# Four linked edits to an attention and two-layer gated feed-forward kernel: rows of a chunk loaded once, omega from two queues, first squares on ScalarE, planner constants

## The chip, the cores and the metric

One core of one Trainium2 chip. The time is device microseconds (us) of one execution; lower is better. Engines: PE (TensorE), DVE (VectorE), ACT (ScalarE), POOL (GpSimd), SP (SyncE, which here only issues DMAs).

## The reference

Attention with random features, then two gated feed-forward blocks, all in float32. B, H, S, D = 4, 8, 576, 64; 128 features; 2304 tokens of width 512; inner width 1536.

```python
scale = 1.0 / np.sqrt(np.sqrt(D))
def phi(x):                       # x is q * scale or k * scale
    proj = np.einsum('bhsd,md->bhsm', x, omega)
    h = proj - np.sum(x * x, axis=-1, keepdims=True) / 2.0
    return np.exp(h - np.max(h, axis=-1, keepdims=True)) / np.sqrt(m)
kv = np.einsum('bhsm,bhsd->bhmd', k_p, v)
z = np.sum(k_p, axis=2)
num = np.einsum('bhsm,bhmd->bhsd', q_p, kv)
out = num / (np.einsum('bhsm,bhm->bhs', q_p, z)[..., None] + 1e-06)
x = out.transpose(0, 2, 1, 3).reshape(B * S, H * D)
x = (silu(x @ w_gate) * (x @ w_val)) @ w_out
return ((x @ w_a) * (x @ w_b)) @ w_out2
```

## The kernel before

The tokens go through in five chunks of 512 (the last has 256). A chunk needs the attention of its tokens, for four pairs of heads (NP = 4), and then the two feed-forward blocks (layer(c, 0) and layer(c, 1), lines 756 and on). Every feed-forward product is made of three matmuls, since a float32 factor is split into a high and a low part in the format fp32r (lines 768 to 770). The input x and the inner rows h are split by ACT (high part: xh, hh) and DVE (low part: xl, hl), the weights likewise (wh on line 748, wl through sub on line 320).

Weights arrive as float64 bits, 512 KB a tile, on SP's queue (line 724); two ACT operations (727, 730) and two DVE operations (733, 736) make float32 of them. Half of the tiles are converted in the first chunk, half in the first and again in the second; a converted tile is written back to DRAM (kept, line 742), and later chunks load that (line 746).

The attention of the next chunk runs beside the feed-forward blocks of the present one. For a pair of heads, keys() (478) and queries() (537) load the transposed rows (xT, by loads() on 464), the tokens (kt, qt) and values (vt), all on SP's queue, and call features() (364). That squares the tokens in place on POOL (line 376), sums them on DVE (378, 381), projects the rows on PE (411 or 436), takes maxima on DVE (446), forms a bias (449, 453) and takes exponentials on ACT (458). The keys' features are then multiplied with the values on PE (ps_kv, line 495).

How the rows are multiplied with omega depends on the chunk:

- WHOLE (chunk 0): float32 rows times bd, a 128x256 block-diagonal of omega, one matmul a tile (line 436). bd is filled by two DMAs of omega from ACT's queue (338) and two memsets (341).
- SPLIT (chunk 1): rows split in high and low part (rs, 396 and 399), times bdh and bdl (353, 355), three matmuls.
- STACKED (chunks 2 to 4): for each head of the pair, one tile rs holds the high part of its 64 rows on one half of the partitions and the low part on the other, times oms (both parts of omega side by side, copied by POOL on line 359), one matmul a tile (411). For this loads() fetches the 64 rows of a head twice, to both halves of a tile xT; ACT rounds all 128 partitions (388) and POOL subtracts on the upper half (391, through 320). A pair takes four tiles xT, two for the keys and two for the queries; the ring has four (261).

The order of the instructions on each engine is not written by hand. All operations are recorded with an engine, an estimated duration and a due time, and Plan.order() (97) plays them through: whichever engine is free next takes, of its operations whose inputs are there by then, the one with the earliest due time. An operation's result is there SIGNAL us after its end; a DMA occupies a common pipe at RATE (in MB per us). ACT pays TABLE for a change of its function table. The due times of the layers begin at ALONE and are spaced by the estimated PE time (at(), 331); a raw weight load may not be planned earlier than EARLY us ahead of its due time. Estimates of POOL are 0.2 + 0.0023 us an element, of ACT 0.09 + n/1200, of DVE 0.07 + n/960. The order found is then issued; on the chip each engine and queue keeps to it and waits on semaphores.

Of the kernel before, what the change touches and what calls it, by code (L numbers as in the profile page):

```python
# [9 lines left out]
F32 = mybir.dt.float32  # L10
# [46 lines left out]
class Plan:  # L57
# [5 lines left out]

    SIGNAL = 0.06
    TABLE = 1.4
    RATE = 0.26

    def __init__(self):  # L70
        self.ops = []
# [25 lines left out]
    def order(self):  # L97
# [4 lines left out]
            for b in o.bufs:  # L102
                b.left = b.ops
        engines = (PE, ACT, DVE, POOL, SP)
        free = dict.fromkeys(engines, 0.0)
        coming = {e: [] for e in engines}
        waiting = {e: [] for e in engines}
        held = {}
# [86 lines left out]
def attention_moe_moe(ctx: ExitStack, tc: tile.TileContext, qT, kT, q, k, v, omegaT,  # L195
# [124 lines left out]
        eng.tensor_tensor(out=out, in0=a, in1=hi.bitcast(F32), op=ALU.subtract)  # L320


    ALONE = 44.0
    EARLY, LATE = 26.0, 3.0
    FFN, BESIDE = 0.2258 / 512, 28.0
    n_ffn = 3 * (2 * NF * KD + NF * KD)
# [8 lines left out]

    def constants():
        for h in range(2):
            on(ACT, dma(32), -1e6, lambda h=h: nc.scalar.dma_start(
                out=bd.tile[h * D:(h + 1) * D, h * M:(h + 1) * M], in_=omegaT),
                writes=[(bd, (h, h))])  # L340
            on(DVE, dve(M), -1e6, lambda h=h: nc.vector.memset(
                bd.tile[h * D:(h + 1) * D, (1 - h) * M:(2 - h) * M], 0.0),
                writes=[(bd, (h, 1 - h))])
        on(DVE, dve(1), -1e6, lambda: nc.vector.memset(warm.tile, 0.0), writes=[(warm,)])
        on(ACT, act(1), -1e6, lambda: nc.scalar.activation(
            out=warm.tile, in_=warm.tile, func=AF.Exp), writes=[(warm,)], table="exp")
        on(POOL, dict(pace=0.6), -1e6, lambda: make_identity(nc, ident.tile), writes=[(ident,)])
        for i, t in enumerate(r_vt.tiles):
            on(POOL, pool(650), -1e6, lambda t=t: nc.gpsimd.memset(t, 1.0), writes=[(ones, i)])
        for i, t in enumerate(r_kp.tiles):  # L350
            on(POOL, pool(128), 20, lambda t=t: nc.gpsimd.memset(
                t[:, :, 1].bitcast(F32), 0.0), writes=[(zeros, i)])
        on(DVE, dve(256), 20, lambda: nc.vector.tensor_copy(bdh.tile, bd.tile),
           reads=[(bd, *bd.state)], writes=[(bdh,)])
        on(DVE, dve(256), 20, lambda: sub(nc.vector, bdl.tile, bd.tile, bdh.tile),
           reads=[(bd, *bd.state), (bdh,)], writes=[(bdl,)])
        for i, x in enumerate((bdh, bdl)):
            for h in range(2):
                on(POOL, pool(M), 25, lambda i=i, x=x, h=h: nc.gpsimd.tensor_copy(
                    oms.tile[h * D:(h + 1) * D, i], x.tile[h * D:(h + 1) * D, h * M:(h + 1) * M]),  # L360
                    reads=[(x,)], writes=[(oms, (i, h))])


    def features(rT, tok, nt, step, f, due, length, how, psum):

# [5 lines left out]

        def square():
            x = tok.tile[:, 0:nt].rearrange("p t c -> p (t c)")
            nc.gpsimd.tensor_tensor(out=x, in0=x, in1=x, op=ALU.mult)
        on(POOL, pool(nt * P), due - 4, square, writes=[(tok,)])
        on(DVE, dve(nt * P), due - 2, lambda: nc.vector.tensor_reduce(
            out=s.tile[:, 0:nt], in_=tok.tile[:, 0:nt].rearrange("p t (h d) -> p t h d", h=2),
            op=ALU.add, axis=AX.X), reads=[(tok,)], writes=[(s,)])  # L380
# [4 lines left out]
        for h in range(2 if how == STACKED else 0):  # L385
            rs = r_rs.buf()
            stacks.append(rs)
            on(ACT, act(width), due - 4, lambda rs=rs, h=h: nc.scalar.activation(  # L388
                out=rs.tile[:, 0:width], in_=rT[h].tile[:, 0:width], func=AF.Copy),
                reads=[(rT[h], *rT[h].state)], writes=[(rs,)])  # L390
            on(POOL, pool(width), due - 3, lambda rs=rs, h=h: sub(
                nc.gpsimd, rs.tile[D:P, 0:width], rT[h].tile[D:P, 0:width],
                rs.tile[D:P, 0:width]), reads=[(rT[h], *rT[h].state)], writes=[(rs,)])
        if how == SPLIT:
            hi, lo = r_rs.buf(), r_rs.buf()
            on(ACT, act(width), due - 4, lambda: nc.scalar.activation(
                out=hi.tile[:, 0:width], in_=rT[0].tile[:, 0:width], func=AF.Copy),
                reads=[(rT[0], *rT[0].state)], writes=[(hi,)])
            on(POOL, pool(width), due - 3, lambda: sub(
                nc.gpsimd, lo.tile[:, 0:width], rT[0].tile[:, 0:width], hi.tile[:, 0:width]),  # L400
                reads=[(rT[0], *rT[0].state), (hi,)], writes=[(lo,)])
        for g in range(0, nt, 2):
            n = min(2, nt - g)
            mx, top, bias = r_mx.buf(), r_top.buf(), r_bias.buf()
# [2 lines left out]
            if how == STACKED:  # L407
                for t in range(g, g + n):
                    ps = psum.buf()
                    for h in range(2):  # L410
                        on(PE, pe(0.12), d, lambda h=h, ps=ps, t=t: nc.tensor.matmul(  # L411
                            ps.tile[:, 256 * h:256 * (h + 1)],
                            lhsT=stacks[h].tile[:, step * t:step * t + P],
                            rhs=oms.tile.rearrange("p t m -> p (t m)"), start=True, stop=True),
                           reads=[(stacks[h],), (oms, *oms.state)], writes=[(ps, h)])

                    def half(i, ps=ps):
                        return ps.tile.rearrange("p (h t m) -> p h t m", h=2, t=2)[:, :, i]
                    on(ACT, act(256, 0, True), d, lambda half=half, t=t: nc.scalar.activation(
                        out=f.tile[:, t], in_=half(0), func=AF.Copy),  # L420
                       reads=[(ps, 0, 1)], writes=[(f, (t, 0), (t, 1))])
                    on(DVE, dve(256), d, lambda half=half, t=t: nc.vector.tensor_tensor(
                        out=f.tile[:, t], in0=f.tile[:, t], in1=half(1), op=ALU.add),
                       reads=[(ps, 0, 1)], writes=[(f, (t, 0), (t, 1))])
                keys_of = [(f, *parts)]
            else:
                ps = psum.buf()
                for i in range(n):
                    def proj(i=i, ps=ps, g=g):
                        c = slice(step * (g + i), step * (g + i) + P)  # L430
                        out = ps.tile[:, 256 * i:256 * (i + 1)]
                        terms = ([(hi.tile[:, c], bdh.tile), (hi.tile[:, c], bdl.tile),
                                  (lo.tile[:, c], bdh.tile)] if how == SPLIT else
                                 [(rT[0].tile[:, c], bd.tile)])
                        for j, (w, x) in enumerate(terms):
                            nc.tensor.matmul(out, lhsT=w, rhs=x, start=j == 0,  # L436
                                             stop=j == len(terms) - 1)
                    on(PE, pe(0.36 if how == SPLIT else 0.45), d, proj,
                       reads=[(hi,), (lo,), (bdh,), (bdl,)] if how == SPLIT else
                       [(rT[0], *rT[0].state), (bd, *bd.state)], writes=[(ps, i)])  # L440
                keys_of = [(ps, *range(n))]

            def h_of(ps=ps, g=g, n=n):
# [17 lines left out]
                   reads=[(bias,)] if how == STACKED else [(bias,), (ps, t - g)],  # L461
                   writes=[(f, (t, h))], table="exp")

    def loads(rT, src, p, due, how, pieces):

        for h, x in enumerate(rT):
            for b, a, z, at_ in pieces:
                for i in range(len(rT)):
                    rows_ = slice(h * D, (h + 1) * D) if how == STACKED else slice(0, P)
                    to = slice(i * D, (i + 1) * D) if how == STACKED else slice(0, P)  # L470
                    on(SP, dma((z - a) / 2 / len(rT)), due - 9, lambda x=x, b=b, a=a, z=z,
                       at_=at_, to=to, rows_=rows_: nc.sync.dma_start(
                           out=x.tile[to, at_:at_ + z - a], in_=src[b, p][rows_, a:z]),
                       writes=[(x, (i, b))])

    sums, spread = {}, {}

    def keys(b, p, due, length, how):

        rT, tok, vt = [r_xT.buf() for _ in range(2 if how == STACKED else 1)], r_kt.buf(), r_vt.buf()  # L480
        loads(rT, kT, p, due, how, [(b, 0, S, 0)])
        on(SP, dma(320), due - 8, lambda: nc.sync.dma_start(out=tok.tile, in_=bass.AP(
            k.tensor, k.offset + (b * S) * DM + p * P, [[DM, P], [TS * DM, KT], [1, P]])),
            writes=[(tok,)])
# [2 lines left out]
                                               [[DM, P], [TS * DM, KT], [1, P]])),  # L487
           reads=[(ones, 0, 1)], writes=[(vt,)])
        f, kv = r_kf.buf(), ps_k.buf()
        features(rT, tok, KT, TS, f, due, length, how, ps_m if how == WHOLE else ps_p)  # L490
        for t in range(KT):
            for h in range(2):
                r = rows[t]
# [43 lines left out]
    def queries(c, p, due, length, how):  # L537
# [1 line left out]
        t0, t1 = spans[c]  # L539
        n = t1 - t0  # L540
        nt = n // P
        rT, tok = [r_xT.buf() for _ in range(2 if how == STACKED else 1)], r_qt.buf()
        loads(rT, qT, p, due, how,
              [(b, max(t0, b * S) - b * S, min(t1, (b + 1) * S) - b * S, max(t0, b * S) - t0)
               for b in range(t0 // S, (t1 - 1) // S + 1)])
        on(SP, dma(n / 2), due - 8, lambda: nc.sync.dma_start(
# [331 lines left out]
```

## Time and profile before

| | |
|---|---|
| median of 3 runs (lowest, highest) | 1073.5 us (1070.06, 1074.39) |
| profiled execution | 1073.3 us, its span 1071.5 us |
| mean granted clock of PE over the span | 0.992 |
| instructions | 16062 |
| DMA traffic | 177.01 MB, mean 165 GB/s |
| ACT table loads | 24 of 1.28 us |

The span is what the profile covers; the execution has 1.8 us around it. A busy time is the sum of the time in which an engine had an instruction running. "idle before <-" names what an engine's instruction waited for last. An entry like xT<-kT reads: written tile <- what is read. A granted clock of 1.00 is the full level, 0.50 the lower.

### The profile page before, as it was taken

The page shows a single profiled execution, that of the slowest core. Times are in us where ns is not written, and L with a number is a line of the kernel's source. Part 1 is how long each engine was busy: PE and PEld are TensorE (multiplying, and loading weights), DVE is VectorE, ACT ScalarE, POOL GpSimd, SP SyncE. Part 2 cuts the span into 40 slices and gives each one's busy share as a digit, 9 for nine tenths or more (in the row PEclk, how much of TensorE's full clock was granted, in tenths as well). Part 3 has the DMA queues.
Part 4 walks back from the last instruction along what each step waited for, and adds up shares of the span by engine and source line. Part 5 has one row for each costly group of instructions (what it writes and reads, how often), then busy time and mean ns, then how long its engine had stood idle before and what let it go on. Part 6 is the DMA issues. An engine that isn't in the chain of part 4 may idle for free.

```text
span 1071.5 us, 16062 instructions
## 1 busy us (share of the span) xinstructions
PE 1044.3 (97%) x5444; PEld 891.2 (83%) x5444; DVE 750.1 (70%) x1441; ACT 686.1 (64%) x1437; POOL 173.3 (16%) x150
## 2 busy tenths in 40 slices
PE   7989999999999999979999999999999999999998
PEld 6868787888888887868888888888888888889998
DVE  5899898999766778979654476885544455536663
ACT  3979987888666668676564456665444445437563
POOL 3220020111100042332400042333000110000000
PEclk9999999999999999989999999999999999999999
DMA  6776785776855465754723253333333333246563
GB/s 198 252 242 220 224 278 189 259 239 223 274 186 196 166 212 177 228 163 135 218 89 108 79 148 109 119 108 114 108 107 93 102 89 98 89 121 183 181 185 99
DMA packets 107697, 177.01 MB, mean 165 GB/s; under 512 B 10720, under 2 KB 46688, under 8 KB 107616
## 3 DMA queue, kind: packets, MB, share of 16 engines
q1 hardware_dynamic: 107456, 175.94, 52.7%
q8 instruction: 42, 0.69, 0.2%
q14 instruction: 39, 0.32, 0.1%
q10 hardware_dynamic: 160, 0.07, 0.0%
HBM read 152.37 MB, written 23.59 MB: 164 GB/s over the span
## 4 chain that ended last, share of the span: by engine, by line
PE 76%; ACT 9%; DVE 8%; issue 4%; DMA 2%; SPq 0%; POOL 0%; ACTq 0%; DVEq 0%; POOLq 0%
PE ps_m L769 23%; PE ps_m L768 23%; PE ps_m L770 23%; PE ps_kv L495 2%; ACT w L730 2%; ACT wh L748 2%; PE ps_p L411 2%; DVE w L733 1%; DMA w<-w 1%; ACT w L727 1%; PE ps_t L703 1%; DVE w L736 1%; DVE wl L320 1%; PE ps_p L436 1%; DVE mx L446 1%
## 5 line engine op out<-in xcount | busy, mean ns | idle before, releaser
L320 DVE TENSOR_TENSOR wl<-w,wh 128x512 fp32r<-128x512 f32 x360 | 263.4, 735 | 172.1 <-ACT wh L748 165.0
L768 PE MATMUL ps_m<-xh,wh 128*128 128x512 f32 (+1 forms) x960 | 360.1, 375 | 3.6 <-ACT xh L530 3.1
L769 PE MATMUL ps_m<-xl,wh 128*128 128x512 f32 (+1 forms) x960 | 355.8, 371 | 4.2 <-DVE xl L320 4.2
L770 PE MATMUL ps_m<-xh,wl 128*128 128x512 f32 (+1 forms) x960 | 355.5, 370 | 0.1
L748 ACT ACTIVATE wh<-w 128x512 fp32r<-128x512 f32 x360 | 225.3, 630 | 123.8 <-PE ps_m L769 94.1
L770 PEld LDWEIGHTS ps_m<-xh,wl 128*128 128x128 f32 x960 | 182.1, 190 | 32.2 <-DVE wl L320 1.2
L768 PEld LDWEIGHTS ps_m<-xh,wh 128*128 128x128 f32 x960 | 182.4, 190 | 31.6 <-ACT xh L530 3.8
L769 PEld LDWEIGHTS ps_m<-xl,wh 128*128 128x128 f32 x960 | 182.3, 190 | 31.7 <-DVE xl L320 5.2
L768 PE MATMUL ps_m<-hh,wh 128*128 128x512 f32 (+1 forms) x480 | 180.6, 376 | 0.0
L770 PE MATMUL ps_m<-hh,wl 128*128 128x512 f32 (+1 forms) x480 | 177.2, 369 | 0.0
L769 PE MATMUL ps_m<-hl,wh 128*128 128x512 f32 (+1 forms) x480 | 177.2, 369 | 0.0
L320 POOL TENSOR_TENSOR rs<-xT,rs 64x576 fp32r<-64x576 f32 (+4 forms) x48 | 68.7, 1440 | 522.2 <-ACT rs L388 219.5
L786 ACT ACTIVATE a<-ps_m 128x512 f32<-128x512 f32 (+1 forms) x120 | 66.4, 553 | 71.7 <-PE ps_m L770 71.4
L789 DVE TENSOR_TENSOR h<-a,ps_m 128x512 f32<-128x512 f32 (+1 forms) x120 | 75.6, 630 | 42.4 <-PE ps_m L770 34.8
L770 PEld LDWEIGHTS ps_m<-hh,wl 128*128 128x128 f32 x480 | 90.5, 189 | 15.7
L768 PEld LDWEIGHTS ps_m<-hh,wh 128*128 128x128 f32 x480 | 90.6, 189 | 12.8
L769 PEld LDWEIGHTS ps_m<-hl,wh 128*128 128x128 f32 x480 | 90.7, 189 | 12.5
L792 ACT ACTIVATE hh<-h 128x512 fp32r<-128x512 f32 (+1 forms) x120 | 70.6, 588 | 29.7 <-DVE h L789 27.8
L733 DVE SCALAR_TENSOR_TENSOR w<-w 128x512 uint32<-128x512 uint32 x108 | 77.2, 721 | 13.6 <-ACT w L730 13.5
L320 DVE TENSOR_TENSOR hl<-h,hh 128x512 fp32r<-128x512 f32 (+1 forms) x120 | 79.8, 665 | 7.3 <-ACT hh L792 3.8
L730 ACT ACTIVATE w<-w 128x512 uint32<-128x512 uint32 x108 | 73.1, 685 | 16.7 <-DMA w<-w 16.5
L736 DVE SCALAR_TENSOR_TENSOR w<-w,w 128x512 uint32<-128x512 uint32 x108 | 77.6, 723 | 6.5 <-ACT w L727 6.4
(90 smaller groups left out, 1065.2 us busy)
## 6 DMA issues: line engine op xcount, KB each, us to landing
w<-kept SPq DMA_DIRECT2D x252, 256.0 KB, 2.7
w<-w SPq DMA_DIRECT2D x108, 512.0 KB, 4.4
kept<-w SPq DMA_DIRECT2D x72, 256.0 KB, 4.5
kt<-k_t SPq DMA_DIRECT2D x16, 320.0 KB, 4.5
vt<-v_t SPq DMA_DIRECT2D x16, 320.0 KB, 5.6
xT<-kT SPq DMA_DIRECT2D x32, 144.0 KB, 3.0
qt<-q_t SPq DMA_DIRECT2D x16, 256.0 KB, 4.4
outT<-h SPq DMA_DIRECT2D x16, 256.0 KB, 2.5
```

What stands on the lines that cost most here:

```text
L320: eng.tensor_tensor(out=out, in0=a, in1=hi.bitcast(F32), op=ALU.subtract)
L411: on(PE, pe(0.12), d, lambda h=h, ps=ps, t=t: nc.tensor.matmul(ps.tile[:, 256 * h:256 * (h + 1)], lhsT=stacks[h].tile[:, step * t:step * t ...
L730: on(ACT, act(CW), due - 10, lambda: nc.scalar.activation(out=raw.tile[:, :, 0], in_=raw.tile[:, :, 0], func=AF.Copy, scale=0.875 * 2.0 ** ...
L733: on(DVE, dve(CW), due - 9, lambda: nc.vector.scalar_tensor_tensor(out=raw.tile[:, :, 0], in0=raw.tile[:, :, 1], scalar=0x80000000, in1=ra ...
L736: on(DVE, dve(CW), due - 9, lambda: nc.vector.scalar_tensor_tensor(out=w.tile.bitcast(U32), in0=w.tile.bitcast(U32), scalar=3, in1=raw.til ...
L748: on(ACT, act(CW), due - 7, lambda: nc.scalar.activation(out=hi.tile.rearrange("p a c -> p (a c)"), in_=w.tile, func=AF.Copy), reads=[(w,) ...
L768: nc.tensor.matmul(o, lhsT=hi.tile[:, wi], rhs=a, start=first, stop=False)
L769: nc.tensor.matmul(o, lhsT=hi.tile[:, wi], rhs=b, start=False, stop=False)
L770: nc.tensor.matmul(o, lhsT=lo.tile[:, wi], rhs=a, start=False, stop=last)
L786: on(ACT, act(n, 0, True), due, lambda a=a, ps=ps: nc.scalar.activation(out=a.tile[:, 0:n], in_=ps[0].tile[:, 0:n], func=AF.Silu if m == 0 ...
L789: on(DVE, dve(n), due, lambda a=a, h=h, ps=ps: nc.vector.tensor_tensor(out=h.tile[:, 0:n], in0=a.tile[:, 0:n], in1=ps[1].tile[:, 0:n], op= ...
L792: on(ACT, act(n), due + 2, lambda h=h, hh=hh: nc.scalar.activation(out=hh.tile[:, 0:n], in_=h.tile[:, 0:n], func=AF.Copy), reads=[(h,)], w ...
```

## The change

- The planner: SIGNAL 0.06 to 0.12, engines free from 0.7 us on (START) in place of 0, RATE 0.26 to 0.24, ALONE 44 to 40.
- One half of omega is loaded from SP's queue, as its first DMA, and the other from ACT's.
- The memset of ones covers only the last column of the values' tiles; both memsets are charged less. The kp memsets and the four oms copies on POOL may not be planned before ALONE, the bdh and bdl operations on DVE not before 20 us.
- The squares of the first pair's keys and queries (first) run on ACT.
- STACKED: the rows of both heads come in one tile by one DMA a piece. ACT rounds a head's 64 partitions into the same partitions of rs, POOL subtracts and writes the low part to the other 64. A pair of keys and queries thus takes two tiles xT.

```diff
-    SIGNAL = 0.06
+    SIGNAL = 0.12
+    START = 0.7
-    RATE = 0.26
+    RATE = 0.24
...
-        free = dict.fromkeys(engines, 0.0)
+        free = dict.fromkeys(engines, self.START)
...
-    ALONE = 44.0
+    ALONE = 40.0
...
         for h in range(2):
-            on(ACT, dma(32), -1e6, lambda h=h: nc.scalar.dma_start(
+            eng, issue = ((SP, nc.sync), (ACT, nc.scalar))[h]
+            on(eng, dma(32), -1e6, lambda h=h, issue=issue: issue.dma_start(
...
-            on(POOL, pool(650), -1e6, lambda t=t: nc.gpsimd.memset(t, 1.0), writes=[(ones, i)])
+            on(POOL, dict(pace=0.2), -1e6, lambda t=t: nc.gpsimd.memset(
+                t[:, :, 2 * D:2 * D + 1], 1.0), writes=[(ones, i)])
...
-            on(POOL, pool(128), 20, lambda t=t: nc.gpsimd.memset(
-                t[:, :, 1].bitcast(F32), 0.0), writes=[(zeros, i)])
-        on(DVE, dve(256), 20, lambda: nc.vector.tensor_copy(bdh.tile, bd.tile),
-           reads=[(bd, *bd.state)], writes=[(bdh,)])
+            on(POOL, dict(pace=0.25), 60, lambda t=t: nc.gpsimd.memset(
+                t[:, :, 1].bitcast(F32), 0.0), writes=[(zeros, i)], after=ALONE)
+        on(DVE, dve(256), 30, lambda: nc.vector.tensor_copy(bdh.tile, bd.tile),
+           reads=[(bd, *bd.state)], writes=[(bdh,)], after=ALONE / 2)
...
-                on(POOL, pool(M), 25, lambda i=i, x=x, h=h: nc.gpsimd.tensor_copy(
+                on(POOL, dict(pace=0.35), 60, lambda i=i, x=x, h=h: nc.gpsimd.tensor_copy(
...
-                    reads=[(x,)], writes=[(oms, (i, h))])
+                    reads=[(x,)], writes=[(oms, (i, h))], after=ALONE)
...
-            nc.gpsimd.tensor_tensor(out=x, in0=x, in1=x, op=ALU.mult)
-        on(POOL, pool(nt * P), due - 4, square, writes=[(tok,)])
+            if first:
+                nc.scalar.activation(out=x, in_=x, func=AF.Square)
+            else:
+                nc.gpsimd.tensor_tensor(out=x, in0=x, in1=x, op=ALU.mult)
+        on(*((ACT, act(nt * P)) if first else (POOL, pool(nt * P))), due - 4, square, writes=[(tok,)])
...
-                out=rs.tile[:, 0:width], in_=rT[h].tile[:, 0:width], func=AF.Copy),
-                reads=[(rT[h], *rT[h].state)], writes=[(rs,)])
-            on(POOL, pool(width), due - 3, lambda rs=rs, h=h: sub(
-                nc.gpsimd, rs.tile[D:P, 0:width], rT[h].tile[D:P, 0:width],
-                rs.tile[D:P, 0:width]), reads=[(rT[h], *rT[h].state)], writes=[(rs,)])
+            own_, other = (slice(i * D, (i + 1) * D) for i in (h, 1 - h))
...
+                out=rs.tile[own_, 0:width], in_=rT.tile[own_, 0:width], func=AF.Copy),
+                reads=[(rT, *rT.state)], writes=[(rs, 0)])
+            on(POOL, pool(width), due - 3, lambda rs=rs, own_=own_, other=other: sub(
+                nc.gpsimd, rs.tile[other, 0:width], rT.tile[own_, 0:width],
+                rs.tile[own_, 0:width]), reads=[(rT, *rT.state), (rs, 0)], writes=[(rs, 1)])
...
-    def loads(rT, src, p, due, how, pieces):
...
+    def loads(rT, src, p, due, pieces):
+
+        for b, a, z, to in pieces:
+            on(SP, dma((z - a) / 2), due - 9, lambda b=b, a=a, z=z, to=to: nc.sync.dma_start(
+                out=rT.tile[:, to:to + z - a], in_=src[b, p][:, a:z]), writes=[(rT, b)])
```

## Rows read from the trace of the kernel before

**Rows 1.** The page, busy time, share of the span and count by engine:

```profile
PE 1044.3 (97%) x5444; PEld 891.2 (83%) x5444; DVE 750.1 (70%) x1441; ACT 686.1 (64%) x1437; POOL 173.3 (16%) x150
```

**Rows 2.** Windows: length, busy PE, PEld, DVE, ACT, POOL, clock, DMA share, GB/s:

```profile
100.00:200.00 100.00, 97.22 (x474) 80.72 (x473) 89.95 (x165) 86.56 (x170) 10.29 (x7) 0.98 0.74 238
...
400.00:500.00 100.00, 92.30 (x460) 77.24 (x459) 89.63 (x168) 72.50 (x170) 32.15 (x25) 0.95 0.59 188
```

**Rows 3.** Who waited for whom, PE: us in total, times, longest:

```profile
PE ps_p L411 <- DVE qf L422: 6.9, 2, 6.5
```

**Rows 4.** Timeline of the start: start us, us, engine, line, operation, count [idle before]:

```profile
0.73 1.19 ACTq L338 DMA_DIRECT2D bd<-omegaT  x2
...
4.95 1.25 POOL L376 TENSOR_TENSOR kt<-kt 128x640 f32<-128x640 f32 x1 [2.20 <-DMA kt<-k_t]
...
5.77 0.58 DVE L353 CAST bdh<-bd 128x256 fp32r<-128x256 f32 x1 [4.42 <-DMA bd<-omegaT]
5.78 4.60 PE L436 MATMUL ps_m<-bd,xT 128*128 128x256 f32 x10 [5.78 <-DMA bd<-omegaT]
...
8.48 0.62 POOL L359 CAST oms<-bdh 64x128 fp32r<-64x128 f32 x2
...
10.76 0.81 DVE L378 TENSOR_REDUCE s<-kt 128x10 f32<-128x640 f32 x1
...
13.93 2.17 ACT L458 ACTIVATE kf<-ps_m,bias 128x128 f32<-128x128 f32 x8 [10.48 <-DVE bias L453]
...
14.39 2.25 PE L495 MATMUL ps_kv<-vt,kf 112*128 112x129 f32 x16 [1.46 <-issue]
```

**Rows 5.** DMA issues by line, 0.7 to 1.0, then 1.5 to 2.0: us to landing:

```profile
xT<-kT SPq DMA_DIRECT2D x1, 288.0 KB, 3.0
bd<-omegaT ACTq DMA_DIRECT2D x1, 32.0 KB, 3.3
...
bd<-omegaT ACTq DMA_DIRECT2D x1, 32.0 KB, 4.3
```

**Rows 6.** Chain of waits, 448 to 472: start us, us, what:

```profile
459.31 1.29 POOL rs L320
...
464.33 4.19 DMA w<-w
...
470.30 0.58 PE ps_p L411
```

**Rows 7.** Windows, columns as in rows 2:

```profile
470.00:480.00 10.00, 9.70 (x35) 8.03 (x36) 8.35 (x14) 6.62 (x18) 4.33 (x4) 0.69 0.60 197
...
64.00:66.00 2.00, 2.00 (x6) 1.52 (x6) 2.00 (x6) 0.60 (x1) 0.00 (x0) 0.50 0.08 12
```

**Rows 8.** Timelines of DVE, POOL and PE between 44 and 64:

```profile
44.59 1.28 DVE L733 SCALAR_TENSOR_TENSOR w<-w 128x512 uint32<-128x512 uint32 x2
...
59.09 2.35 DVE L733 SCALAR_TENSOR_TENSOR w<-w 128x512 uint32<-128x512 uint32 x2
...
58.70 1.58 POOL L376 TENSOR_TENSOR kt<-kt 128x640 f32<-128x640 f32 x1 [10.54 <-DVE xt L610]
...
60.38 0.51 PE L768 MATMUL ps_m<-xh,wh 128*128 128x512 f32 x1 [1.31 <-ACT xh L530]
63.54 0.79 PE L769 MATMUL ps_m<-xl,wh 128*128 128x512 f32 x1 [2.66 <-DVE xl L320]
```

**Rows 9.** Timeline of ACT, the operation nearest to a square of a tile:

```profile
43.38 0.70 ACT L396 ACTIVATE rs<-xT 128x576 fp32r<-128x576 f32 x1
```

**Rows 10.** Instructions on the tile xT: duration ns min/median/max, first and last start:

```profile
L472 SPq DMA_DIRECT2D xT<-qT x92: 328/540/1321, 1.6 to 844.3; - x92
...
L472 SPq DMA_DIRECT2D xT<-kT x40: 340/471/1057, 0.7 to 671.1; - x40
```

**Rows 11.** Timeline of SP's issues before the stop at 464:

```profile
457.62 0.32 SPq L746 DMA_DIRECT2D w<-kept  x1
...
460.62 3.67 SPq L472 DMA_DIRECT2D xT<-qT  x6
```

More of the change, by code (lines that the diff above doesn't have):

```diff
@@ L348, in constants @@
         for i, t in enumerate(r_vt.tiles):
-            on(POOL, pool(650), -1e6, lambda t=t: nc.gpsimd.memset(t, 1.0), writes=[(ones, i)])
+            on(POOL, dict(pace=0.2), -1e6, lambda t=t: nc.gpsimd.memset(
+                t[:, :, 2 * D:2 * D + 1], 1.0), writes=[(ones, i)])
         for i, t in enumerate(r_kp.tiles):
-            on(POOL, pool(128), 20, lambda t=t: nc.gpsimd.memset(
-                t[:, :, 1].bitcast(F32), 0.0), writes=[(zeros, i)])
-        on(DVE, dve(256), 20, lambda: nc.vector.tensor_copy(bdh.tile, bd.tile),
-           reads=[(bd, *bd.state)], writes=[(bdh,)])
-        on(DVE, dve(256), 20, lambda: sub(nc.vector, bdl.tile, bd.tile, bdh.tile),
+            on(POOL, dict(pace=0.25), 60, lambda t=t: nc.gpsimd.memset(
+                t[:, :, 1].bitcast(F32), 0.0), writes=[(zeros, i)], after=ALONE)
+        on(DVE, dve(256), 30, lambda: nc.vector.tensor_copy(bdh.tile, bd.tile),
+           reads=[(bd, *bd.state)], writes=[(bdh,)], after=ALONE / 2)
+        on(DVE, dve(256), 30, lambda: sub(nc.vector, bdl.tile, bd.tile, bdh.tile),
            reads=[(bd, *bd.state), (bdh,)], writes=[(bdl,)])
@@ L358, in constants, with features @@
             for h in range(2):
-                on(POOL, pool(M), 25, lambda i=i, x=x, h=h: nc.gpsimd.tensor_copy(
+                on(POOL, dict(pace=0.35), 60, lambda i=i, x=x, h=h: nc.gpsimd.tensor_copy(
                     oms.tile[h * D:(h + 1) * D, i], x.tile[h * D:(h + 1) * D, h * M:(h + 1) * M]),
-                    reads=[(x,)], writes=[(oms, (i, h))])
-    def features(rT, tok, nt, step, f, due, length, how, psum):
+                    reads=[(x,)], writes=[(oms, (i, h))], after=ALONE)
+    def features(rT, tok, nt, step, f, due, length, how, psum, first):
         width = step * (nt - 1) + P
@@ L387, in features @@
             stacks.append(rs)
-            on(ACT, act(width), due - 4, lambda rs=rs, h=h: nc.scalar.activation(
-                out=rs.tile[:, 0:width], in_=rT[h].tile[:, 0:width], func=AF.Copy),
-                reads=[(rT[h], *rT[h].state)], writes=[(rs,)])
-            on(POOL, pool(width), due - 3, lambda rs=rs, h=h: sub(
-                nc.gpsimd, rs.tile[D:P, 0:width], rT[h].tile[D:P, 0:width],
-                rs.tile[D:P, 0:width]), reads=[(rT[h], *rT[h].state)], writes=[(rs,)])
+            own_, other = (slice(i * D, (i + 1) * D) for i in (h, 1 - h))
+            on(ACT, act(width), due - 4, lambda rs=rs, own_=own_: nc.scalar.activation(
+                out=rs.tile[own_, 0:width], in_=rT.tile[own_, 0:width], func=AF.Copy),
[3 more added lines that the diff above has]
+                rs.tile[own_, 0:width]), reads=[(rT, *rT.state), (rs, 0)], writes=[(rs, 1)])
         if how == SPLIT:
@@ L396, in features @@
             on(ACT, act(width), due - 4, lambda: nc.scalar.activation(
-                out=hi.tile[:, 0:width], in_=rT[0].tile[:, 0:width], func=AF.Copy),
-                reads=[(rT[0], *rT[0].state)], writes=[(hi,)])
+                out=hi.tile[:, 0:width], in_=rT.tile[:, 0:width], func=AF.Copy),
+                reads=[(rT, *rT.state)], writes=[(hi,)])
             on(POOL, pool(width), due - 3, lambda: sub(
-                nc.gpsimd, lo.tile[:, 0:width], rT[0].tile[:, 0:width], hi.tile[:, 0:width]),
-                reads=[(rT[0], *rT[0].state), (hi,)], writes=[(lo,)])
+                nc.gpsimd, lo.tile[:, 0:width], rT.tile[:, 0:width], hi.tile[:, 0:width]),
+                reads=[(rT, *rT.state), (hi,)], writes=[(lo,)])
         for g in range(0, nt, 2):
@@ L414, in features @@
                             rhs=oms.tile.rearrange("p t m -> p (t m)"), start=True, stop=True),
-                           reads=[(stacks[h],), (oms, *oms.state)], writes=[(ps, h)])
+                           reads=[(stacks[h], 0, 1), (oms, *oms.state)], writes=[(ps, h)])
                     def half(i, ps=ps):
@@ L433, in proj @@
                                   (lo.tile[:, c], bdh.tile)] if how == SPLIT else
-                                 [(rT[0].tile[:, c], bd.tile)])
+                                 [(rT.tile[:, c], bd.tile)])
                         for j, (w, x) in enumerate(terms):
@@ L439, in features @@
                        reads=[(hi,), (lo,), (bdh,), (bdl,)] if how == SPLIT else
-                       [(rT[0], *rT[0].state), (bd, *bd.state)], writes=[(ps, i)])
+                       [(rT, *rT.state), (bd, *bd.state)], writes=[(ps, i)])
                 keys_of = [(ps, *range(n))]
@@ L462, in features @@
                    writes=[(f, (t, h))], table="exp")
-    def loads(rT, src, p, due, how, pieces):
[L466 to L474, printed above, removed]
+    def loads(rT, src, p, due, pieces):
+        for b, a, z, to in pieces:
+            on(SP, dma((z - a) / 2), due - 9, lambda b=b, a=a, z=z, to=to: nc.sync.dma_start(
+                out=rT.tile[:, to:to + z - a], in_=src[b, p][:, a:z]), writes=[(rT, b)])
     sums, spread = {}, {}
     def keys(b, p, due, length, how):
-        rT, tok, vt = [r_xT.buf() for _ in range(2 if how == STACKED else 1)], r_kt.buf(), r_vt.buf()
-        loads(rT, kT, p, due, how, [(b, 0, S, 0)])
+        rT, tok, vt = r_xT.buf(), r_kt.buf(), r_vt.buf()
+        loads(rT, kT, p, due, [(b, 0, S, 0)])
         on(SP, dma(320), due - 8, lambda: nc.sync.dma_start(out=tok.tile, in_=bass.AP(
@@ L489, in keys @@
         f, kv = r_kf.buf(), ps_k.buf()
-        features(rT, tok, KT, TS, f, due, length, how, ps_m if how == WHOLE else ps_p)
+        features(rT, tok, KT, TS, f, due, length, how, ps_m if how == WHOLE else ps_p,
+                 first=due < 4)
         for t in range(KT):
@@ L541, in queries @@
         nt = n // P
-        rT, tok = [r_xT.buf() for _ in range(2 if how == STACKED else 1)], r_qt.buf()
-        loads(rT, qT, p, due, how,
+        rT, tok = r_xT.buf(), r_qt.buf()
+        loads(rT, qT, p, due,
               [(b, max(t0, b * S) - b * S, min(t1, (b + 1) * S) - b * S, max(t0, b * S) - t0)
@@ L550, in queries @@
         f = r_qf.buf()
-        features(rT, tok, nt, P, f, due, length * 0.5, how, ps_p)
+        features(rT, tok, nt, P, f, due, length * 0.5, how, ps_p, first=due < 8)
         (shared if how == STACKED else own)(c, p, f, due, length)
```

## Prediction

> **What bounds the kernel now.** I began with the busy times: TensorE (PE) is busy for 1044.3 of the span's 1071.5 us [rows 1], so it stood idle for 27.2 us, and that idle time, with what a fallen clock adds, is all that a change of order can win. Next I read the windows, to see where it lies [rows 2]: from 100 to 200 PE lacks 2.8 us at a granted clock of 0.98 (about 2.0 us more); from 400 to 500 it lacks 7.7 us at 0.95. Then the waits of PE, by releaser: one stop of 6.5 us, for VectorE (DVE), is the longest behind the start [rows 3].
>
> **The start.** PE's first matmul begins at 5.78 us, released by the load of omega into bd [rows 4]. Both halves go out from ScalarE's (ACT's) queue, the two issues taking 1.19 us from 0.73. The first half lands 3.3 us after its issue, at 4.03; the second is issued at about 1.31 and lands 4.3 us after that, at 5.6; the first keys' rows, from SP, land 3.0 us after theirs [rows 5]. So the second half of omega is what PE waits for. Then ten projections take 4.60 us, and the gap at 14.39 follows: PE's first key sums wait 1.46 us for the exponentials, which begin at 13.93 and wait for their bias, which needs the sum of squares that DVE takes only at 10.76 [rows 4]. GpSimd (POOL) had the square done at 4.95 + 1.25 = 6.20. What held the sum was DVE's own order, three maxima first: the plan charges POOL 1.67 us for the square and as much for each of the two memsets of ones ahead of it.
>
> **The stop at 464.** The chain of waits shows it whole [rows 6]: a subtraction on POOL ends at 460.60 and frees a tile of rows; SP, which stood behind that, issues rows (xT) in six pieces; only then comes a weight load, at 464.33, whose data passes ACT and DVE and releases PE at 470.30. The clock had fallen meanwhile: 0.69 from 470 to 480 (PE's two levels are 1.2 and 2.4 GHz, so this is a mixture), which costs 10 x 0.31 = 3.1 us [rows 7]. The stop is worth 6.5 + 3.1 = 9.6 us. The same shape stands at 58 to 64: PE stops for 1.31 and 2.66 us, 4.0 us, for the last pair of the first chunk's attention [rows 8], and the clock, at 0.50 (the lower level) from 64 to 66, costs 1.0 us more [rows 7].
>
> **The change, part by part.**
>
> *Omega from two queues.* SP issues one half ahead of the keys' rows, ACT the other. Both now leave at about 0.73 and should land as the first half did, near 4.0. The rows go out one issue later, near 1.3, and with their 3.0 us land at 4.3; PE starts 0.14 behind that or a little later, say 4.5. I take **1.3 us**. Bounds: 1.6 if the rows keep 4.03, nothing if they take the 4.3 us that the second half took. The square's tokens also leave 0.5 us later on SP; they land ahead of the maxima still. The Trainium skill (DMA: Bandwidth & Descriptors, "Issuing engines are not separate DMA queues") says that several issuing engines save only the sequencer's issue time; here that would be half of 1.19 us, 0.6, and the sum below would end 0.7 later. The rows show more than that: the second half left 0.58 us later and landed 1.6 later.
>
> *First squares on ACT.* ACT is idle from its warm-up to 13.93. No row shows a Square; its nearest is the 128x576 copy on ACT, 0.70 us [rows 9]. The work is off POOL, which nobody waited for, so it saves nothing by itself; what counts is that the plan charges it 0.6 us and two memsets of 0.2, so it can put the sum ahead of the maxima. Then bias and exponentials begin near 8, beside the projections. I take the whole gap, **1.46 us**; bounds 0 (the plan keeps its order) and 1.46. Next in line would be the values' load, which no longer waits for long memsets and so goes out earlier.
>
> *Constants put off.* DVE loses two operations at 5.77, 0.58 us for the first and some 1.2 for both, from a stretch with idle time, and gets them after 20 us: the cover is PE's own work there; I count 0, or 1.2 lost without the cover. POOL's four casts (0.62 a pair, 1.24) and memsets (0.35) leave the start and come when the feed-forward layers begin, where DVE is full. The price of that is seen at 59: two DVE operations took 2.35 us there, with a square running on POOL, and 1.28 at 44.59, without one [rows 8]. I count **0.5 us** lost; bounds 0 and 1.1, that ratio applied to 1.59 us. The Trainium skill (GPSIMD Reference, "Key points") says that POOL shares its SBUF interfaces with DVE and collides with instructions of two SBUF inputs; the trace agrees (1.07 us more for the pair). By the rule taken strictly all 1.59 us would be lost and the sum be 1.1 higher.
>
> *Rows loaded once.* There are 92 + 40 = 132 issues of rows [rows 10]; 20 of them belong to chunks 0 and 1 and stay, the 112 others become 28. So SP loses 84 issues of some 0.5 us. More: a pair of keys and queries filled all four tiles, now it takes two, so a load no longer stands behind the subtraction on POOL. SP's last issue ahead of the stop ended at 457.62 + 0.32 = 457.94; without the 2.7 us of standing up to 460.62 and the 3.67 of issuing six pieces [rows 11], the weight load leaves 464.33 - 457.94 = 6.4 us earlier, if its own tile is free, against a stop of 6.5. I take the whole **9.6 us**. Bounds: 0, if another wait holds the same queue, and 11.2, with the other stop of the same releaser (6.9 - 6.5 = 0.4 [rows 3]) and what else PE lacks from 400 to 500 (7.7 - 6.5 = 1.2 [rows 2]). ACT's copy has half the partitions and the same columns, so the same time. The subtraction now writes the other half of the partitions; no row has that. The one in the chain took 1.29 us of what the profile shows [rows 6], the slowest POOL square of like size 1.58 [rows 8]; even twice that for each of 40 would find room on a POOL that is busy a third of 400 to 500 [rows 2]. I take 0, bounds 0 and, where PE waits for the last of a pair, 1.3 us for each of eight pairs, 10.
>
> *The plan with later signals, slower loads, and a first layer due at 40.* All orders on all engines change. Of what mere order costs now, 4.0 + 1.0 us at 58 to 66 and 2.8 + 2.0 from 100 to 200 can go: 9.8 us. As much may come new. No row prices it; I take **0**, bounds 9.8 either way.
>
> The sum goes against the profiled execution, 1073.3 us (span 1071.5 and 1.8 around it), 0.2 under the median: 1073.3 - 1.3 - 1.5 + 0.5 - 9.6 = 1061.4, against the median some **1061.5 us**.
>
> **The rivals.** A measurement of this kernel tells about 0.5%, 5.4 us, from none, so faster is below 1068.1 and slower above 1078.9.
>
> *The order's own stops go too.* Against the median: take 5.0 (the stop at 58) off: 1056.5; all 9.8: 1051.7. For it: later signals place a consumer later, and the stops at 58 to 64 and 100 to 200 are engines standing behind one operation too early in their order. Against it: DVE is full there, and an order cannot add an engine. Chance 0.12.
>
> *Another load takes the place.* Tokens (kt, qt) have one tile each and stay on SP; if a weight load stands behind them as it did behind rows, the 9.6 us don't come: 1071.1. For it: the same queue, as at 464. Against it: one such load per pair, not six in a row. Chance 0.19.
>
> *The start does not gain.* PE waits for the rows instead of omega, and DVE keeps its maxima ahead: 1064.3. That is also the case in which the change doesn't do what it says at the start, and it holds the case of the issue time alone (1062.2). Chance 0.06.
>
> *Slower: the plan of the first chunk starves an engine.* DVE is busy 90% and ACT 87% from 100 to 200 [rows 2], splitting each weight. The plan now believes in 0.24 MB/us for loads where it believed 0.26, and the trace moves about 0.24 there, so planned loads run late and work on weights is queued behind the next chunk's attention. DVE has 10.05 us to spare in those 100, some 20 over the chunk of 200; an order that idles it by more makes it the bound, and every us beyond, less the 12 won, is lost. It decides from 1078.9 - 1061.5 = 17.4 us of new stops; four of the size of 100 to 200 (4.8) are 19: 1061.5 + 19 = 1080.5. Against it: the chunk now stops for 4.8 us in 100. Chance 0.11.
>
> **How the numbers follow.** The forecast (1056 to 1067) has 0.52. The chances: faster 0.52 + 0.12 + 0.06 = 0.70; same 0.19; slower 0.11. The range reaches from the far end of the first rival, 1051, past the second's 1071.1 by the late bounds of its start (1.3 + 1.5), to 1074, and leaves out the slower one.
>
> **What would show it.** First matmul at about 4.5, exponentials before 10, no gap before the key sums; SP's row issues 48; no stop of PE over 3 us between 360 and 500 and a granted clock of 1.00 from 460 to 490; POOL's casts after 38. Wrong it would be if PE's idle time in 0 to 20 stays over 6.5 us, if a weight load still stands behind another load on SP, or if 60 to 270 shows new stops beyond 5 us.

## The result, and the profile after

The changed kernel takes 1058.8 us (median of 4 runs, 1056.96 to 1061.38), the kernel before 1073.8 beside it: the ratio is 0.9868, 95% interval 0.9849 to 0.9888. 1061.5 was forecast, in 1051 to 1074. Its profiled execution took 1058.15 us, with a span of 1056.4, 15.1 under that of before.

The page's busy times and the windows, columns as in [rows 1] and [rows 2]:

```profile
PE 1039.0 (98%) x5444; PEld 887.8 (84%) x5444; DVE 748.8 (71%) x1441; ACT 686.6 (65%) x1433; POOL 170.4 (16%) x148
```

```profile
100.00:200.00 100.00, 100.00 (x512) 84.34 (x512) 92.79 (x172) 81.16 (x162) 14.29 (x8) 1.00 0.76 245
...
390.00:400.00 10.00, 7.56 (x33) 6.00 (x33) 8.82 (x17) 6.53 (x16) 4.95 (x4) 0.89 0.56 166
400.00:410.00 10.00, 10.00 (x54) 8.55 (x54) 7.21 (x16) 8.18 (x18) 1.83 (x2) 0.94 0.50 171
...
470.00:480.00 10.00, 10.00 (x53) 8.41 (x52) 9.77 (x21) 7.46 (x18) 4.08 (x3) 1.00 0.49 157
...
60.00:62.00 2.00, 2.00 (x5) 1.61 (x6) 1.39 (x3) 1.98 (x4) 0.00 (x0) 0.50 0.74 247
62.00:64.00 2.00, 2.00 (x7) 1.54 (x7) 0.69 (x1) 1.49 (x3) 0.00 (x0) 0.70 0.84 248
```

PE now idles 1056.4 - 1039.0 = 17.4 us (27.2 before). Read window by window: 100 to 200 is full at a granted clock of 1.00, where 2.8 us and the clock lacked; 470 to 480 has its clock back (0.69 in [rows 7]); but the stop from 390 to 400 has grown, with a lower clock behind it, and the clock behind 60 is as low as it was. In the kernel before, that stop was 1.2 us:

```profile
405.79 0.50 PE L769 MATMUL ps_m<-xl,wh 128*128 128x512 f32 x1 [1.19 <-DVE xl L320]
```

How far each kernel had come is read best from the stores of finished chunks. SP's timeline, the last store of chunk 0 and of chunk 1, first before, then after:

```profile
298.03 0.34 SPq L816 DMA_DIRECT2D outT<-h  x1
...
535.52 0.34 SPq L816 DMA_DIRECT2D outT<-h  x1
```

```profile
289.20 0.34 SPq L818 DMA_DIRECT2D outT<-h  x1
...
520.04 0.34 SPq L818 DMA_DIRECT2D outT<-h  x1
```

8.8 us were won by the end of chunk 0, 15.5 by the end of chunk 1, and nothing after. So more than half of the gain lies ahead of the stop at 464. Who waited for whom, PE, the longest:

```profile
PE ps_m L443 <- DMA xT<-kT: 4.6, 1, 4.6
PE ps_m L771 <- DVE xl L321: 2.9, 2, 2.4
PE ps_t L621 <- DVE xt L612: 1.9, 1, 1.9
...
PE ps_p L418 <- DVE qf L429: 0.7, 1, 0.7
```

The last row answers to [rows 3]: of the stop of 6.5 us 0.7 are left. The 2.4 us in the second are the grown stop at 396. The third, with two more waits behind it, is the stop at 58, 1.9 + 0.7 + 0.4 = 3.0 us. Before, the same three waits were 0.6, 1.3 and 2.7 us, 4.5 together; [rows 8] has the last two, and the first is

```profile
58.63 0.44 PE L619 MATMUL ps_t<-ident,xt 128*128 128x128 f32 x2 [0.56 <-DVE xt L610]
```

The start, in the timeline and in the DMA landings, answers to [rows 4, 5]:

```profile
0.73 0.58 ACTq L340 DMA_DIRECT2D bd<-omegaT  x1
...
0.74 0.57 SPq L340 DMA_DIRECT2D bd<-omegaT  x1
...
1.36 0.57 SPq L474 DMA_DIRECT2D xT<-kT  x1
...
4.63 4.35 PE L443 MATMUL ps_m<-bd,xT 128*128 128x256 f32 x10 [4.63 <-DMA xT<-kT]
...
5.54 0.74 ACT L380 ACTIVATE kt<-kt 128x640 f32<-128x640 f32 x1 [2.69 <-DMA kt<-k_t]
...
9.02 0.81 DVE L384 TENSOR_REDUCE s<-kt 128x10 f32<-128x640 f32 x1
...
10.75 2.69 ACT L465 ACTIVATE kf<-ps_m,bias 128x128 f32<-128x128 f32 x10 [1.28 <-DVE bias L460]
...
11.22 0.46 PE L497 MATMUL ps_kv<-vt,kf 112*128 112x129 f32 x2 [0.51 <-issue]
```

```profile
xT<-kT SPq DMA_DIRECT2D x1, 288.0 KB, 3.1
...
bd<-omegaT ACTq DMA_DIRECT2D x1, 32.0 KB, 2.3
bd<-omegaT SPq DMA_DIRECT2D x1, 32.0 KB, 2.1
```

PE waits for the keys' rows instead of omega and starts 1.15 us earlier. The sum of squares still starts only after two maxima, 9.02, though ACT had the square at 5.54 + 0.74 = 6.28; the key sums follow with 0.5 us of waiting.

Last, SP and POOL ahead of the place where the stop was, the timeline of each:

```profile
451.19 0.81 SPq L474 DMA_DIRECT2D xT<-qT  x2
452.04 0.43 SPq L726 DMA_DIRECT2D w<-w  x1
```

```profile
448.20 2.96 POOL L321 TENSOR_TENSOR rs<-xT,rs 64x512 fp32r<-64x512 f32 x2 [10.85 <-ACT rs L395]
```

This contradicts the prediction: a row load still stands behind POOL's subtractions. They end at 448.20 + 2.96 = 451.16, the load goes at 451.19, and the weight load behind it at 452.04. PE hardly stops all the same (0.7 us from 450 to 460).

### The profile page after: what moved, and what is told of

Its sections match the earlier page's. It is cut to its first block, busy times and chain, and to the rows that moved or that the text cites. A ratio compares the mean times of both kernels' runs of the same rounds, so it can differ in the third digit from the quotient of the medians.

```text
span 1056.4 us, 15912 instructions
## 1 busy us (share of the span) xinstructions
PE 1039.0 (98%) x5444; PEld 887.8 (84%) x5444; DVE 748.8 (71%) x1441; ACT 686.6 (65%) x1433; POOL 170.4 (16%) x148
## 4 chain that ended last, share of the span: by engine, by line
PE 87%; DVE 7%; ACT 3%; issue 2%; DMA 1%; SPq 0%; DVEq 0%; ACTq 0%
PE ps_m L771 26%; PE ps_m L772 26%; PE ps_m L770 26%; PE ps_kv L497 3%; PE ps_p L418 2%; PE ps_p L443 1%; PE ps_t L705 1%; DVE w L738 1%; DVE wl L321 1%; PE ps_t L587 1%; DVE mx L453 1%; PE ps_t L679 1%; DVE w L735 1%; PE ps_m L443 1%; DVE h L791 0%
## 5 line engine op out<-in xcount | busy, mean ns | idle before, releaser
L321 POOL TENSOR_TENSOR rs<-xT,rs 64x576 fp32r<-64x576 f32 (+4 forms) x48 | 63.7, 1327 | 536.2 <-issue 203.7
L321 DVE TENSOR_TENSOR hl<-h,hh 128x512 fp32r<-128x512 f32 (+1 forms) x120 | 77.3, 644 | 6.1 <-ACT hh L794 2.7
```

## The experiments

All ratios are to the kernel before, measured on the same chip beside each; kernels are compared by their ratios. Every kernel in which the planner gets other numbers is ordered anew on all engines; where "own order" is said, every engine's order is the same as in the kernel named.

| kernel | us | ratio, 95% interval |
|---|---|---|
| changed kernel | 1058.8 | 0.9868 (0.9849 to 0.9888) |
| E1 rows edit alone | 1071.8 | 0.9995 (0.9979 to 1.001) |
| E2 planner constants alone | 1074.2 | 1.0024 (1.0005 to 1.0044) |
| E3 start alone | 1074.5 | 1.0022 (1.001 to 1.0035) |
| E4 all but the rows edit | 1066.9 | 0.9949 (0.993 to 0.9968) |
| E5 changed, four issues a row load, own order | 1059.5 | 0.9879 (0.9849 to 0.9908) |
| E6 changed, a pair holds four tiles | 1062.3 | 0.9912 (0.9884 to 0.994) |
| E7 changed, omega from one queue, own order | 1056.5 | 0.9858 (0.9831 to 0.9885) |
| E8 changed, squares on POOL, own order | 1056.3 | 0.9861 (0.9826 to 0.9897) |
| E9 before, own order, row loads behind weights on SP | 1068.4 | 0.9959 (0.9941 to 0.9976) |
| E10 changed, SIGNAL 0.18 | 1066.4 | 0.9939 (0.9923 to 0.9954) |
| E11 changed, SIGNAL 0.06 | 1072.1 | 0.9995 (0.9985 to 1.0004) |
| E12 changed, SIGNAL 0.13 | 1062.8 | 0.9908 (0.9886 to 0.993) |

**E1 to E3: each part alone.** The edits are the hunks of the diff above: E1 those of loads(), keys(), queries() and STACKED; E2 SIGNAL, START, RATE and ALONE; E3 constants() and the squares.

> The kernel before with the rows edit alone. Theory A (the parts as the prediction priced them): the stop of 6.5 us at 464 and the fallen clock behind it go, 9.6 us, so 1064 us. Theory B (the plan's later signals, slower loads and earlier due time make the gain, and the rows matter only as one more change of order): 1073 us, within 3.

> The kernel before with SIGNAL, START, RATE and ALONE of the changed one, nothing else. Theory A: no gain of its own, 1074 us, within 5. Theory B: most of the 15 us, 1062 us or less.

> The kernel before with omega from two queues, the first squares on ScalarE and the constants put off, planner constants and rows as before. Theory A: first matmul near 4.6 us, the gap ahead of the key sums shorter, 2.3 us gained, 1071.5 us. Theory B: the same at the start, but lost again in the new order, 1074 us.

None of the three gains; E2 and E3 lose 0.2%. Theory B falls with E2, theory A with E1. E1 shows why. Its chain of waits, and SP's last issue ahead of it in the timeline, are

```profile
458.50 1.29 POOL rs L320
...
459.87 1.30 POOL rs L320
...
461.19 0.33 SPq L468
...
461.57 4.36 DMA w<-w
...
468.31 0.58 PE ps_p L412
```

```profile
456.82 0.32 SPq L741 DMA_DIRECT2D w<-kept  x1
```

This is the chain of [rows 6] again: subtraction, row load, weight load, PE. One piece of rows has taken the place of six, so the weight load leaves 2.8 us earlier, at 461.57. But SP stands longer ahead of the rows: 4.0 us, from 457.14 to 461.19, where it stood 2.7. The two heads now share a tile, so the load waits for both subtractions (to 461.17); in the kernel before it waited for the first alone (to 460.60, [rows 6]). PE's stop is 5.4 us. E3 has the best start of all: first matmul at 4.55, the sum of squares behind one maximum only, first key sums at 10.60 without a gap. It has no gain in the end; its new order has stops of 3.35 us at 473 and 2.42 at 294.

**E4: two of the three parts.**

```diff
-        rT, tok, vt = r_xT.buf(), r_kt.buf(), r_vt.buf()
+        rT, tok, vt = [r_xT.buf() for _ in range(2 if how == STACKED else 1)], r_kt.buf(), r_vt.buf()
...
```

> The changed kernel without the rows edit: each head's rows are again loaded twice. Theory A: the stop behind the row issues comes back, 1058.8 + 9.6 = 1068.4 us, with one stop of PE of 4 us or more between 360 and 500. Theory B: 1059 to 1062 us.

0.5% gained by two parts neither of which gains alone, and 0.8% more with the third. The time agrees with A, but not the place. PE's longest stop there is 2.5 us, not 4, and E4 is behind long before it; its last stores of chunk 0 and of chunk 1:

```profile
295.03 0.34 SPq L823 DMA_DIRECT2D outT<-h  x1
...
528.99 0.34 SPq L823 DMA_DIRECT2D outT<-h  x1
```

Against the changed kernel 5.8 us are lost by the end of chunk 0, and 9.0 by the end of chunk 1.

**E5 and E6: what the rows edit saves.**

```diff
-    def loads(rT, src, p, due, pieces):
-
+    def loads(rT, src, p, due, pieces, cuts=1):
+        C = P // cuts
...
-            on(SP, dma((z - a) / 2), due - 9, lambda b=b, a=a, z=z, to=to: nc.sync.dma_start(
-                out=rT.tile[:, to:to + z - a], in_=src[b, p][:, a:z]), writes=[(rT, b)])
+            on(SP, dma((z - a) / 2), due - 9, lambda b=b, a=a, z=z, to=to: [nc.sync.dma_start(
+                out=rT.tile[C * i:C * i + C, to:to + z - a], in_=src[b, p][C * i:C * i + C, a:z]) for i in range(cuts)], writes=[(rT, b)])
...
-        loads(rT, kT, p, due, [(b, 0, S, 0)])
+        loads(rT, kT, p, due, [(b, 0, S, 0)], 4 if how == STACKED else 1)
...
```

> The changed kernel in its own order on every engine, but each load of rows of the stacked chunks is issued as four of 32 partitions, so SP issues 84 row loads more, as before, with the same bytes. If the saving lies in SP's issue time: 84 issues of some 0.5 us are back ahead of weight loads, 1062 to 1068 us, with a stop of PE behind a weight load between 360 and 500. If it lies in the tiles that a pair no longer fills (a load no longer stands behind POOL's subtraction): 1059 us, within 2.

```diff
+        rT.spare = r_xT.buf() if how == STACKED else None
...
-                reads=[(rT, *rT.state)], writes=[(rs, 0)])
+                reads=[(rT, *rT.state), (rT.spare, *rT.spare.state)], writes=[(rs, 0)])
...
```

> The changed kernel, but a pair of keys and queries of a stacked chunk again holds all four tiles xT (each of its two tiles holds a second one idle until the subtractions have read it), with one issue a piece. All engines' orders are planned anew. If the saving lies in the tiles: a weight load stands behind a row load that waits for POOL, 1064 us or more. If it lies in the issue time: 1059 us, within 3.

The 84 issues are worth nothing that can be measured in this order: in E5 SP spends 4.31 us on one batch of eight row issues at 449.07, the weight load behind them goes 1.4 us later than in the changed kernel, and the time is the same (0.9879 against 0.9868). E6 lies between: 0.4% more than the changed kernel, with intervals that just overlap, a stop of 2.4 us, and another order. It doesn't settle whether the tiles or the order cost that.

**E7 and E8: the start in the changed kernel's own order.**

```diff
-            on(eng, dma(32), -1e6, lambda h=h, issue=issue: issue.dma_start(
+            on(eng, dma(32), -1e6, lambda h=h: nc.scalar.dma_start(
```

> The changed kernel with both halves of omega issued from ScalarE's queue as before; the order of all else is unchanged on every engine. The rows' load leaves SP 0.6 us earlier, the second half of omega 0.6 us later. If two queues are worth what was priced: first matmul at 5.6 to 5.9 us and about 1 us lost, 1060 us. If only the issue time counts: first matmul at 5.2 or earlier, 1059.4 us. If the start is hidden behind the later stop at 56: no difference, 1058.8 us.

```diff
-                nc.scalar.activation(out=x, in_=x, func=AF.Square)
+                nc.gpsimd.tensor_tensor(out=x, in0=x, in1=x, op=ALU.mult)
```

> The changed kernel with the first pair's two squares executed on POOL, at the places in the order that they have on ScalarE; the order on PE, DVE and SP is unchanged. If what counted is that the plan puts the sum of squares earlier on DVE, and not the engine: POOL ends the first square at about 6.8 instead of 6.3 us, the sum still starts at 9.0, and the time is the same, 1059 us, within 1. If the engine itself counts: key sums about 0.5 us later, 1059.5 us.

Neither shows in the time, but the time can't show so little: E7's interval of 0.27% is 2.9 us either way. The traces say more. In E7 PE's first matmul is back at 5.38 us, released by omega:

```profile
0.74 0.38 SPq L474 DMA_DIRECT2D xT<-kT  x1
...
0.74 1.19 ACTq L340 DMA_DIRECT2D bd<-omegaT  x2
...
5.38 4.04 PE L443 MATMUL ps_m<-bd,xT 128*128 128x256 f32 x10 [5.38 <-DMA bd<-omegaT]
```

```profile
bd<-omegaT ACTq DMA_DIRECT2D x1, 32.0 KB, 3.3
...
bd<-omegaT ACTq DMA_DIRECT2D x1, 32.0 KB, 3.9
```

The second fence has the landings of the two halves. The first matmul is 0.75 us later than in the changed kernel. The ten projections end 9.42 - 8.98 = 0.44 us later, PE goes on behind its wait for xt at 58.49 instead of 57.85, 0.64 later, and the last store of chunk 0 stands at 289.63, 0.43 later. So in this trace the stop at 58 doesn't hide the later start. But traces of one order differ by as much (in E5 that store stands at 290.45), so what the start is worth in the total stays open.

In E8 POOL takes 1.25 us for the square from 5.98, and the sum starts at 9.35 behind the same two maxima: it doesn't wait for the square. The next operation on DVE, though, stands beside POOL's square of the queries:

```profile
10.10 1.04 POOL L380 TENSOR_TENSOR qt<-qt 128x512 f32<-128x512 f32 x1 [2.87 <-DMA qt<-q_t]
...
10.40 0.76 DVE L387 TENSOR_SCALAR nsq<-s 128x10 f32<-128x10 f32 x1
...
12.15 0.46 PE L497 MATMUL ps_kv<-vt,kf 112*128 112x129 f32 x2 [0.47 <-issue]
```

It took 0.16 us in the changed kernel. The key sums come 0.93 us later than there, 0.33 of it because the sum itself starts later. So at the start the engine counts for about 0.6 us, which was the second of the two expectations; the total can't show it.

**E9: the stop at 464 in the kernel before, in its own order.** Only SP's queue differs: a row load of the stacked chunks goes behind the next two raw weight loads.

```diff
...
-        for o in self.order():
-            o.fn()
+        todo = self.order()
+        for o in [x for x in todo if x.rows]:
+            i = todo.index(o)
+            last = min(todo.index(u) for u in o.users)
+            after = [k for k in range(i + 1, last) if todo[k].eng == SP and todo[k].size == 0.5][:2]
+            if len(after) == 2:
+                todo.insert(after[1], todo.pop(i))
+        for o in todo:
+            o.fn()
...
-                       writes=[(x, (i, b))])
+                       writes=[(x, (i, b))]).rows = how == STACKED
```

> The kernel before with its own order on PE, DVE, ScalarE and POOL; only in SP's queue each row load of the stacked chunks is moved behind the next two raw weight loads. If the stop at 464 comes from the weight load standing behind row loads that wait for POOL: the stop shrinks from 6.5 us to under 1.5, and the time falls by 7 to 10 us, to 1062 to 1066 us. If the queue only shows what ScalarE's and DVE's order makes late anyway: a stop of 4 us or more stays and the time is 1070 us or more.

Between the two: the weight load leaves at 456.38 instead of 464.33, and of the 6.5 us of stop 3.85 stay. The chain of waits now ends in the engines' own queues. Behind it, from the timelines, stand the weight load on SP, and ACT's half of a conversion and the stop of PE:

```profile
462.94 0.69 DVE h L796
...
463.65 0.64 ACT hh L799
...
464.92 0.69 DVE w L740
465.61 0.34 DVE qf L429
...
465.99 0.56 PE ps_p L418
```

```profile
456.38 0.43 SPq L731 DMA_DIRECT2D w<-w  x1
```

```profile
464.19 0.66 ACT L737 ACTIVATE w<-w 128x512 uint32<-128x512 uint32 x1
...
465.99 0.56 PE L418 MATMUL ps_p<-oms,rs 128*128 128x256 f32 x1 [3.85 <-DVE qf L429]
```

PE needs a PSUM tile, which frees when DVE has taken qf; that stands in DVE's order behind a conversion of weights, whose ACT half stands in ACT's order behind hh, which waits for DVE's h. So the queue held 2.7 us of the stop. Behind the shorter stop the clock is back sooner: 0.83 from 460 to 470 and 1.00 from 470 to 480, where 0.69 stood. Together that is 4.4 us of the total, 0.4%, clear of the noise. The rest of the stop was order.

**E10 to E12: SIGNAL in the changed kernel.**

```diff
-    SIGNAL = 0.12
+    SIGNAL = 0.18
```

> The changed kernel with SIGNAL 0.18 in place of 0.12, so all orders are planned anew. If later signals as such give better orders: 1059 us or less. If an order's stops are mostly a matter of chance: 1054 to 1070 us, with stops at other places.

> The changed kernel with SIGNAL 0.06 as before; START, RATE, ALONE and all other parts as changed. If later signals as such give better orders: 1065 us or more. If it is a matter of chance: anywhere from 1054 to 1070 us.

> The changed kernel with SIGNAL 0.13 in place of 0.12, a difference of 10 ns in the plan that means nothing by itself. If the value matters: 1059 us, within 1.5. If the order is a matter of chance: over 2 us from it, either way, with the larger stops of PE at other places.

With 0.06 the whole gain is gone: PE's waits of E11 begin with

```profile
PE ps_p L418 <- DVE qf L429: 7.0, 4, 2.8
PE ps_m L443 <- DMA xT<-kT: 4.9, 1, 4.9
PE ps_t L621 <- DVE xt L612: 3.9, 2, 3.7
```

though rows, omega and squares are as changed. All three later signals are better than that. But 10 ns more in the plan (0.12 to 0.13) cost 0.4%, and 0.18 costs 0.7% against 0.12, each with its stops at other places: later signals help here, and how much is partly the chance of one order.

All kernels with an order of their own say the same. The five with both the start edits and a later signal gain (the changed one, E4, E6, E10, E12: 0.9868 to 0.9949); the four that lack one or both do not (E1, E2, E3, E11: 0.9995 to 1.0024). The 0.8% that the rows edit adds (E4 to the changed kernel) are hardly more than the 0.7% by which the orders with all edits differ among themselves (0.9868 to 0.9939).

## Why the prediction was right, and where it was not

The time, its sign and its size came out: 14.9 us gained where 12 were forecast. The working behind it holds only in part. Its terms put 1.3 + 1.5 - 0.5 = 2.3 us ahead of the end of chunk 0 and 9.6 between that and the end of chunk 1; by the stores, 8.8 and 6.7 were won.

**Omega from two queues.** Right in the trace (first matmul at 4.63, forecast 4.5; 1.15 us for 1.3), not shown as a term of the sum: E7 takes 0.75 of it back, and a loss of that size is below what the time can tell. Over all traces the first matmul stands at 4.54 to 4.95 with two queues (nine traces) and at 5.38 to 6.26 with one (five). The halves landed after 2.1 and 2.3 us, not 3.3 as in [rows 5], so both were there before the rows; with one queue again, in E7, they took 3.3 and 3.9. By the Trainium skill (DMA: Bandwidth & Descriptors, "Issuing engines are not separate DMA queues") only the sequencer's issue time, about 0.6 us, would be saved. The traces show more, 1.0 us on the mean of the first matmuls.

**First squares.** That the sum's place on DVE comes from the plan's charge, and not from a faster square, is what E8 shows. That the engine itself saves nothing is not borne out: with the squares on POOL the key sums came about 0.6 us later. And the sum was put ahead of one maximum of three, not of all: the gap fell from 1.46 us to 0.5 ahead of the first key sums and 0.3 behind them, half of what was taken. E3 had no gap and no gain.

**Constants put off.** The 0.5 us could not be told apart in any run. POOL's casts stand at 44.00, as expected. The two DVE operations had taken 0.58 + 0.43 = 1.0 us, not 1.2.

**Rows loaded once: the step that failed.** It said that a load "no longer stands behind the subtraction on POOL". It does, in E1 and in the changed kernel. With four tiles to two pairs the planner only loads rows earlier, for a later pair, until the ring is full again, and the next load waits for the next subtractions, now those of both heads. And it gave the whole stop to SP's queue, since the chain of waits led there; E9 shows 2.7 us of 6.5, and 4.4 us in all where 9.6 were taken. The issues were worth nothing in the changed order (E5), and 2.8 us of the weight load's time but 1.1 of the stop in E1's. That the stop is gone all the same goes with the order: PE's wait for qf at that place is 6.5 us before, 5.4 in E1 and E2, 3.35 in E3, 2.5 in E4 and 0.7 in the changed kernel, and E2 to E4 don't have the rows edit.

**The plan: the term taken as 0.** Alone it is 0 or a small loss (E2), as taken; together with the other edits it decides, since with SIGNAL 0.06 the other edits give nothing (E11). From E11 to the changed kernel SIGNAL alone is worth 1.3%, over the bound of 9.8 us. Of the stops of mere order the one in 100 to 200, 2.8 + 2.0 us, went, as the first rival had it; the one at 58 stayed, 3.0 us and 1.6 of clock for 4.5 and 1.3 (the prediction left out its first wait, and the clock of 0.87 from 66 to 68); the one at 405 grew from 1.2 to 2.4, with 1.7 of clock behind it. The forecast held because a term sized too large (rows) and one sized too small (order) made up for each other, which is luck.

**The rivals.** That another load takes the place is what E1 shows, with the same kind of load; in the changed kernel it stands there too and does no harm in that order. The slower one did not come: 100 to 300 is full.

What stays open: which property of the order the later signals improve, why they do so only beside the start edits, and whether the step from E4 to the changed kernel (0.9949 to 0.9868) is the rows' free tiles or chance. For that one needs the rows edit in a fixed order, which was not tried, since the order depends on the tiles.

## What to carry to other kernels

Where a planner writes the order, an edit has two effects, what it saves and the order it brings; run it in a fixed order (E5, E7, E8, E9) before you credit it, and change a constant by an amount that means nothing (E12) to see how far orders alone scatter; here one such change made 0.4%. A term of 1 us is below what times with an interval of 0.3% can tell; it is read in the traces, over several of them. A chain of waits names one way back; before you price a stop by it, ask what would hold the same instruction if that link were gone, here two in-order engines just behind. Parts that gain nothing alone can gain together, so test them in both directions, alone and left out.

## What the runs showed of the hardware that was not expected

The first ten projections took 3.88 us in E11 (4.88 to 8.76) and 4.60 in the kernel before, E5 and E8, the same instructions on the same data with a granted clock of 1.00 in the window's row; six of the same shape took 1.46 us later (changed kernel, at 23.28), 0.24 apiece against 0.39 to 0.46. So PE is slow at first in a way that the granted clock does not show, by an amount that varies by 0.7 us, more than half of what an earlier start brought.

DVE's nsq, 128x10 elements or fewer, took 0.16 us as a rule. In the changed kernel four of its 36 took over 0.3, and each of the four ended 0.03 us behind an operation of POOL that had started before it. One of them:

```profile
45.55 1.25 POOL L382 TENSOR_TENSOR kt<-kt 128x640 f32<-128x640 f32 x1
```

```profile
45.60 1.23 DVE L387 TENSOR_SCALAR nsq<-s 128x8 f32<-128x8 f32 x1
```

The others took 1.22 (at 189.70), 1.25 (268.63) and 0.60 us (502.94); the 0.76 us in E8 above ended in the same way. The square of 128x640 took 0.74 us on ACT and 1.25 on POOL. POOL's subtraction into the other half of the partitions took what the old one did: 2.96 us for two of 64x512, against 3.09.
